# Second w_in's pieces decoded at an even rate, each tied on VectorE behind the evacuation of its feed-forward step

## Chip, cores and metric

The kernel runs on 1 core of one Trainium2 chip. The metric is device time in microseconds (us) of one execution; lower is better. Before the change three runs gave 786.98, 778.69 and 790.01 us (median 786.98).

## What is computed

Attention over 2 batches x 8 heads x 768 tokens x 64, in which a query sees the keys that were assigned to the same of 16 centroids, and then two feed-forward layers on the 1536 tokens of 512 features (d_ff is 2048):

```python
mask = q_assign[:, :, :, None] == k_assign[:, :, None, :]
scores = np.where(mask, scale * np.matmul(q, k.transpose(0, 1, 3, 2)), -1e9)
attn = softmax(scores)
x = np.matmul(attn, v)                  # 1536 x 512, after a transpose
h = x @ moe_w_in
g = np.maximum(h, 0.0) + np.log1p(np.exp(-np.abs(h)))
x = g @ moe_w_out
h = x @ moe2_w_in                       # the second w_in
g = np.maximum(0.01 * h, h)
out = g @ moe2_w_out
```

## The kernel before

The weights arrive as 64-bit floats. A piece of a weight is 128 x 512 numbers: SyncE loads its words into one of two staging buffers (`st`), VectorE puts an f32 together from them in three instructions (`decode`, L141, L144, L147), ScalarE rounds it to f16 (the high half) and VectorE subtracts to get the low half. All matrix products run as three f16 products, high x high, high x low and low x high.

The work stands in this order. The sixteen heads of attention come first; beside them the first layer's two weights are decoded, and from the ninth head on the first feed-forward layer runs interleaved with attention. That layer goes over four blocks of 384 tokens: (batch 0, tokens 0), (0, 384), (1, 0), (1, 384). Each block has

- `layer_in`: 16 steps of 12 matmuls (L576). After each step ScalarE evacuates the bank twice (`g_h`, L451, and f32 `mr`, L452), and VectorE subtracts them (`g_l`, L453). These four lines are `act_pair`'s.
- `layer_mid`: 4 outputs of 48 matmuls each (L589), which read all 16 pairs `g_h`, `g_l`, one pair after the other, three matmuls per pair. Each output is evacuated by ScalarE (`xth`, L593) and VectorE (`xtl`, L594).

A generator yields after each step of `layer_in` and four times in each output of `layer_mid`, so that a block has 32 yields; after each yield other work may be issued. Six PSUM banks turn among these steps once attention is done (`mps_next`), and `mr` has two buffers.

When attention is done, `w2` is opened and the second w_in (`moe2_w_in`) is queued: 16 pieces, in four groups of four quarters (`quad_pieces`). Each quarter is decoded (three VectorE instructions). The second layer's first product is computed with seven products in place of eight, for which sums and differences of quarters are needed: in each group GpSimd makes four differences (L209, L213, L215, L218), and ScalarE and VectorE split seven matrices into halves (L198, L199). GpSimd also makes the sums of the left side, `left_sums(0)`: 28 instructions (L485 and L183), with eight casts on ScalarE (`sh`, L182) in between; they need outputs of both blocks of batch 0. Then comes `layer_in2` (L521) and `layer_out` (L609).

What sets the order: every instruction is issued with a priority, and the compiler puts each engine's instructions into one fixed order. An engine then works through its order and waits where an input is not there. Feed-forward step n has priority 8 + 0.25 n. `w2_step`, called once after each yield, gives the v-th step of the second w_in the priority 17 + 0.9 v (`W2_PRI`), whatever step calls it; it finishes one piece (`convs.pop(0)()`) and starts the load of another. After the block (0, 384) a loop calls it until no piece is left.

In what follows "the second block" is (0, 384) and "the third block" is (1, 0). Line numbers are those of the kernel before; in the kernel after, the lines from L453 on stand 2 or 3 lines lower (L453 is L455, L485 is L487, L593 is L595, L594 is L596).

Of the kernel before, what the change touches and what calls it, by code (L numbers as in the profile page):

```python
# [13 lines left out]
ALU = mybir.AluOpType  # L14
# [31 lines left out]

W_FREE, W_FROM, W_TO, W_PER = 4, 8, 10, 5
W_PRI = ((0, 0.5), (17, 0.3))
W2_PRI = (17, 0.9)
O2_PRI = (38, 0.3)  # L50
S_PRI = 30

# [6 lines left out]
def attn_moe_kernel(  # L59
# [13 lines left out]
    V, S, G, PE = nc.vector, nc.scalar, nc.gpsimd, nc.tensor  # L73
# [94 lines left out]
    def in_pieces(w, wh, wl):  # L168
        wi = w.bitcast(I32)
        for f in range(DFF // 512):  # L170
            for kk in range(KDM):
                cs = slice(f * 512, (f + 1) * 512)
                src = wi[kk * 128:(kk + 1) * 128, f * 1024:(f + 1) * 1024]
                yield partial(w_piece, wh[:, kk, cs], wl[:, kk, cs], src)

    def out_pieces(w, wh, wl, order=None):
        wi = w.bitcast(I32)
        for kk in order or range(KFF):
            yield partial(w_piece, wh[:, kk, :], wl[:, kk, :], wi[kk * 128:(kk + 1) * 128, :])
# [245 lines left out]
    late, w2 = {}, {}  # L425
# [16 lines left out]
    def mps_next():  # L442
        if pmx[0] is pm:
            turn["m"] = 1 - turn.get("m", 0) if not (wq or convs) else 1
            return pm.tile([128, 512], F32, tag=f"m{turn['m']}", name="m")
        return pmx[0].tile([128, 512], F32, tag="m", name="m")

    def act_pair(m, hp, func, scale, alpha, g=("h", "l"), tag="mr"):
        r = late["mt"].tile([128, TB], F32, tag=tag, name=tag)
        gh, gl = (late[n][:, m, :] for n in g)  # L450
        S.activation(out=gh, in_=hp, func=func, scale=scale, alpha=alpha)  # L451
        S.activation(out=r, in_=hp, func=func, scale=scale, alpha=alpha)  # L452
        V.tensor_tensor(out=gl, in0=r, in1=gh, op=ALU.subtract)  # L453

    def act_softplus(m, hp):  # L455
        act_pair(m, hp, AF.Softplus, 1.0 / (WS * XS), 0.0)
# [13 lines left out]
    def act_leaky(m, hp, g, tag):  # L470
        act_pair(m, hp, AF.Prelu, 1.0 / WS, 0.01, g, tag)
# [92 lines left out]
    def layer_in(b, t0, act, wh, wl):  # L564
        xh, xl = xt_h[b], xt_l[b]
        ts = slice(t0, t0 + TB)
        for m in range(KFF):
            hp = mps_next()[:, 0:TB]
            ms = slice(m * 128, (m + 1) * 128)
            ops = []  # L570
            for kk in range(KDM):
                ops += [(wh[:, kk, ms], xh[:, kk, ts]), (wh[:, kk, ms], xl[:, kk, ts])]
            for kk in range(KDM):
                ops += [(wl[:, kk, ms], xh[:, kk, ts])]
            for i, (w_, x_) in enumerate(ops):
                PE.matmul(out=hp, lhsT=w_, rhs=x_, start=(i == 0), stop=(i == len(ops) - 1))  # L576
            act(m, hp)
            yield

    def layer_mid(b, t0):  # L580
        xh, xl = xt_h[b], xt_l[b]
        ts = slice(t0, t0 + TB)
        for m in range(KDM):
            yp = mps_next()[:, 0:TB]
            ms = slice(m * 128, (m + 1) * 128)
            n = 0
            for kk in range(KFF):
                for w_, g_ in ((w_outh, late["h"]), (w_outh, late["l"]), (w_outl, late["h"])):
                    PE.matmul(out=yp, lhsT=w_[:, kk, ms], rhs=g_[:, kk, :], start=(n == 0), stop=(n == 3 * KFF - 1))  # L589
                    n += 1  # L590
                if kk % 4 == 3:
                    if kk == KFF - 1:
                        S.activation(out=xh[:, m, ts], in_=yp, func=AF.Copy, scale=1.0 / WS)  # L593
                        V.scalar_tensor_tensor(  # L594
                            out=xl[:, m, ts], in0=yp, scalar=1.0 / WS, in1=xh[:, m, ts], op0=ALU.mult, op1=ALU.subtract  # L595
                        )  # L596
                    yield
# [20 lines left out]
    def pri(x):  # L618
        return int(100000 + 10000 * x)
# [4 lines left out]
    @contextmanager  # L624
    def at_pri(x):
        old = tc.cur_priority
        tc.cur_priority = pri(x)
        yield
        tc.cur_priority = old
# [8 lines left out]
    with at_pri(-9):  # L638
# [6 lines left out]
            out=ss[:, 1:2], in0=ss[:, 0:1], scalar1=ss[:, 2:3], scalar2=ss[:, 1:2], op0=ALU.mult, op1=ALU.add  # L645
# [30 lines left out]
    wq = list(in_pieces(w_in1, w_inh, w_inl))  # L676
    convs = []
    wtie = {"h": -1}

    cnt = {"w": 0, "v": 0, "m": 0}  # L680

    def w_step():
        w0, wr = W_PRI[cnt["w"] >= 34]
# [14 lines left out]
        cnt["w"] += 1  # L698

    def w2_step():  # L700
        with at_pri(W2_PRI[0] + W2_PRI[1] * cnt["v"]):
            if convs:
                convs.pop(0)()
            if wq:
                convs.append(wq.pop(0)())
        cnt["v"] += 1

    def m_steps(g):
        for _ in g:
# [4 lines left out]
    def moe1():  # L714
        wq.extend(out_pieces(w_out1, w_outh, w_outl))
        for b in range(B):
            for t0 in range(0, SEQ, TB):
                for _ in layer_in(b, t0, act_softplus if b or t0 else act_ln_exp, w_inh, w_inl):
                    if len(w2):
                        w2_step()  # L720
                    else:
                        w_step()
                    yield
                while (b, t0) == (0, 0) and (wq or convs):
                    w_step()
                if (b, t0) == (1, TB):
                    late["h2"], late["l2"] = (
                        w.rearrange("p k f -> p (k f)")[:, 0:KFF * TB].rearrange("p (k t) -> p k t", t=TB)
                        for w in (w_outh, w_outl)
                    )  # L730
                    order = [kk + 4 * r for kk in range(4) for r in range(4)]
                    wq.extend(out_pieces(w_out2, w_out2h, w_out2l, order))
                    for i in range(KFF + 1):
                        with at_pri(O2_PRI[0] + O2_PRI[1] * i):
                            if convs:
                                convs.pop(0)()
                            if wq:
                                convs.append(wq.pop(0)())
                for _ in layer_mid(b, t0):
                    if len(w2):  # L740
                        w2_step()
                    else:
                        w_step()
                    yield
                if (b, t0) == (0, TB):
                    while wq or convs:
                        w2_step()
                    with at_pri(S_PRI):
                        left_sums(0)

    def moe2():
        for b in range(B):
# [3 lines left out]
            for t0 in range(0, SEQ, TB):  # L756
                yield from layer_out(b, t0, w_out2h, w_out2l)

    ff = m_steps(moe1())

    def chain(h):
# [91 lines left out]
```

## Time and profile before

| what | us |
|---|---|
| three runs | 786.98, 778.69, 790.01 (median 786.98) |
| the profiled execution | 782.94 |
| its span, first to last instruction | 780.7 |
| TensorE matmul busy | 703.5 (90%) |
| VectorE busy | 435.0 (56%) |
| ScalarE busy | 352.1 (45%) |
| GpSimd busy | 303.7 (39%) |
| mean granted TensorE clock | 0.965 of full speed |

PE is TensorE, DVE is VectorE, ACT is ScalarE, POOL is GpSimd. Busy shares are means over stages with different limits: what counts is where TensorE, which runs the longest chain, stands idle or gets a lower clock, and who released it.

### The profile page before, as it was taken

Reading aid. Unit: us, or ns where it says so; the run is one execution under the profiler, and the core shown is the slowest. Engines: PE = TensorE matmul, PEld = TensorE weight load, DVE = VectorE, ACT = ScalarE, POOL = GpSimd, SP = SyncE. Lnnn points to the kernel's source line nnn. Section 1 sums busy time; section 2 is a strip of 40 time slices with the busy share of each in tenths; the row PEclk is TensorE's granted clock in tenths of the full one; section 3 lists DMA queues with packets and bytes.
Section 4 is the critical chain, followed back from the end, with each engine's and each line's share of the span. In section 5 each row is a group of like instructions: output and inputs, shape, how many; then the busy total and the mean of one; then the engine's idle time right before and its main releaser. Section 6 shows DMA issues by size and latency. Waiting matters only on the chain.

```text
span 780.7 us, 14239 instructions
## 1 busy us (share of the span) xinstructions
PE 703.5 (90%) x5712; PEld 420.6 (54%) x5712; DVE 435.0 (56%) x863; ACT 352.1 (45%) x831; POOL 303.7 (39%) x280
## 2 busy tenths in 40 slices
PE   1788988798798878899798999999999999999998
PEld 1365656455465555566454566666665444665443
DVE  4778757677787777319897411885566000565000
ACT  5375656477776646125433511532665201565000
POOL 5265656568688666303447800000115800111000
PEclk9999889999989989999899999999999999999999
DMA  8967566847675854212343000341000000000000
GB/s 197 183 137 146 120 109 129 167 101 169 173 158 136 162 123 129 93 20 79 113 139 103 1 1 1 108 162 55 1 1 1 27 28 28 1 1 1 27 28 27
DMA packets 104883, 66.03 MB, mean 85 GB/s; under 512 B 90993, under 2 KB 95089, under 8 KB 104817
## 3 DMA queue, kind: packets, MB, share of 16 engines
q1 hardware_dynamic: 104816, 65.13, 34.9%
q8 instruction: 44, 0.72, 0.4%
q14 instruction: 23, 0.18, 0.1%
HBM read 43.02 MB, written 3.15 MB: 59 GB/s over the span
## 4 chain that ended last, share of the span: by engine, by line
PE 61%; DMA 14%; DVE 12%; ACT 6%; issue 2%; POOL 2%; SPq 2%; ACTq 0%; DVEq 0%; POOLq 0%
PE m L609 16%; PE m L521 14%; PE m L589 12%; PE m L576 9%; DMA tk<-nk 3%; DMA v<-in_v_dram 3%; DMA tm<-nq 3%; DVE mm L310 2%; DMA t<-n 2%; DMA st<-in_moe_w_in_dram 2%; DVE w_in2l L199 2%; ACT p L343 2%; PE s L303 2%; PE s L336 1%; PE s L337 1%
## 5 line engine op out<-in xcount | busy, mean ns | idle before, releaser
L345 POOL TENSOR_TENSOR pl<-p 128x768 f16<-128x768 f32 x80 | 117.3, 1473 | 56.7 <-ACT p L343 29.3
L310 DVE TENSOR_REDUCE mm<-s 128x1 f32<-128x384 f32 x190 | 100.2, 550 | 34.7 <-PE s L303 32.2
L524 POOL TENSOR_TENSOR u<-u,p 128x384 f32<-128x384 f32 x16 | 18.2, 1137 | 224.1 <-DVE u L524 212.8
L576 PE MATMUL m<-xth,w_inh 128*128 128x384 f16 x256 | 85.9, 336 | 6.5 <-DVE xtl L594 3.3
L589 PE MATMUL m<-g_h,w_outh 128*128 128x384 f16 x256 | 85.1, 332 | 5.4 <-ACT g_h L451 2.3
L589 PE MATMUL m<-g_l,w_outh 128*128 128x384 f16 x256 | 84.9, 332 | 2.2 <-DVE g_l L453 2.2
L576 PE MATMUL m<-xtl,w_inh 128*128 128x384 f16 x256 | 85.9, 336 | 0.2 <-DMA xtl<-xnl 0.2
L343 ACT ACTIVATE p<-s 128x384 f32<-128x384 f32 x144 | 67.2, 494 | 40.8 <-PE s L337 32.9
L589 PE MATMUL m<-g_h,w_outl 128*128 128x384 f16 x256 | 84.9, 332 | 0.0
L303 PE MATMUL s<-tk,tq 80*128 80x384 f16 x190 | 64.1, 365 | 16.6 <-DMA tk<-nk 9.1
L576 PEld LDWEIGHTS <-w_inh 128*128 128x128 f16 x512 | 50.9, 100 | 42.5 <-issue 11.6
L589 PEld LDWEIGHTS <-w_outh 128*128 128x128 f16 x512 | 50.4, 99 | 40.6 <-issue 5.9
L337 PE MATMUL s<-tm,tk 81*128 81x384 f16 x160 | 53.9, 346 | 10.7 <-DMA tm<-nq 10.6
L336 PE MATMUL s<-t 128*128 128x384 f16 x160 | 54.8, 346 | 7.2 <-ACT p L343 6.5
L521 PEld LDWEIGHTS <-w_in2h 128*128 128x128 f16 x448 | 43.8, 98 | 29.5
L453 DVE TENSOR_TENSOR g_l<-mr,g_h 128x384 f16<-128x384 f32 x64 | 42.0, 659 | 30.2 <-ACT mr L452 30.1
L576 PE MATMUL m<-xth,w_inl 128*128 128x384 f16 x256 | 53.7, 334 | 0.0
L372 PE MATMUL x<-v,p 128*128 128x65 f16 x528 | 50.3, 198 | 1.5 <-DVE y L409 1.5
L373 PE MATMUL x<-v,p 128*128 128x64 f16 x528 | 51.0, 196 | 0.0
L614 ACT ACTIVATE ob<-m 128x512 f32<-128x512 f32 x12 | 7.2, 597 | 91.9 <-PE m L609 91.9
L451 ACT ACTIVATE g_h<-m 128x384 f16<-128x384 f32 x80 | 39.3, 491 | 15.8 <-PE m L576 8.0
L372 PEld LDWEIGHTS <-p 128*128 128x128 bf16 x528 | 40.7, 101 | 3.7 <-issue 1.1
(148 smaller groups left out, 1587.5 us busy)
## 6 DMA issues: line engine op xcount, KB each, us to landing
st<-in_moe_w_in_dram SPq DMA_DIRECT2D x32, 512.0 KB, 4.3
st<-in_moe_w_out_dram SPq DMA_DIRECT2D x32, 512.0 KB, 4.0
qk<-in_q_dram SPq DMA_DIRECT2D x16, 192.0 KB, 3.2
qk<-in_k_dram SPq DMA_DIRECT2D x16, 192.0 KB, 3.8
v<-in_v_dram SPq DMA_DIRECT2D x16, 192.0 KB, 4.2
out_dram<-ob SPq DMA_DIRECT2D x12, 256.0 KB, 2.0
t<-n SPq DMA_TRANSPOSE x16, 4.2
tq<-nq SPq DMA_TRANSPOSE x16, 3.0
```

Source lines behind the costliest of these rows:

```text
L303: PE.matmul(out=o, lhsT=t[0:KS1, c, :], rhs=tk[0:KS1, 3 * j:3 * j + 3, :], start=True, stop=True,)
L310: V.reduce_max(out=mms[h % 2][:, c, j:j + 1], in_=bank[:, 0:3 * 128], axis=AX)
L336: PE.matmul(out=o, lhsT=t1[:, kt, 1, :], rhs=t1[:, 3 * j:3 * j + 3, 0, :], start=True, stop=False)
L337: PE.matmul(out=o, lhsT=t2[0:KS2, kt, :], rhs=tqh[0:KS2, 3 * j:3 * j + 3, :], start=False, stop=True)
L343: S.activation(out=p[:, j, :], in_=sp, func=AF.Exp, scale=scale)
L345: G.tensor_tensor(out=pl, in0=p, in1=pb, op=ALU.subtract)
L372: PE.matmul(out=o, lhsT=pb[:, cs], rhs=v2[:, kt, D:2 * D + 1], start=(kt == 0 and c == 0), stop=False)
L373: PE.matmul(out=o[:, 0:D], lhsT=pb[:, cs], rhs=v2[:, kt, 0:D], start=False, stop=False)
L521: PE.matmul(out=bank, lhsT=w_, rhs=x_, start=(first and i == 0), stop=(i == 5), skip_group_check=True)
L576: PE.matmul(out=hp, lhsT=w_, rhs=x_, start=(i == 0), stop=(i == len(ops) - 1))
L589: PE.matmul(out=yp, lhsT=w_[:, kk, ms], rhs=g_[:, kk, :], start=(n == 0), stop=(n == 3 * KFF - 1))
L609: PE.matmul(out=op, lhsT=g_[:, kk, rs], rhs=w_[:, kk, :], start=(n == 0), stop=(n == 3 * KFF - 1))
```

## The change

`W2_PRI` goes. `w2_step` now counts the feed-forward yields and finishes pieces at an even rate, 17 steps over 60 yields, so that the decode runs from the second block to the end of the third. The instructions of a piece that stand on VectorE are put behind the last evacuation that VectorE was given (`tie["dve"]`, the `g_l` or `xtl` of the step just issued); that is an order within VectorE's queue, not a wait on another engine. The load of the next piece is issued with a priority two heads earlier. The loop that finished all pieces after the second block goes.

```diff
@@ -46,7 +46,7 @@
-W2_PRI = (17, 0.9)
+W2_STEPS = 60
@@ -445,12 +445,14 @@
+    tie = {}
+
     def act_pair(m, hp, func, scale, alpha, g=("h", "l"), tag="mr"):
...
-        V.tensor_tensor(out=gl, in0=r, in1=gh, op=ALU.subtract)
+        tie["dve"] = V.tensor_tensor(out=gl, in0=r, in1=gh, op=ALU.subtract)
@@ -591,7 +593,7 @@
-                        V.scalar_tensor_tensor(
+                        tie["dve"] = V.scalar_tensor_tensor(
@@ -677,7 +679,7 @@
-    cnt = {"w": 0, "v": 0, "m": 0}
+    cnt = {"w": 0, "v": 0, "w2": 0, "m": 0}
@@ -698,12 +700,15 @@
     def w2_step():
-        with at_pri(W2_PRI[0] + W2_PRI[1] * cnt["v"]):
+        cnt["v"] += 1
+        while cnt["w2"] * W2_STEPS < 17 * cnt["v"] and (wq or convs):
             if convs:
-                convs.pop(0)()
+                with tc.issue_after(tie["dve"].ins):
+                    convs.pop(0)()
             if wq:
-                convs.append(wq.pop(0)())
-        cnt["v"] += 1
+                with at_pri(tc.cur_priority / 10000 - 10 - 2):
+                    convs.append(wq.pop(0)())
+            cnt["w2"] += 1
@@ -743,8 +748,6 @@
                 if (b, t0) == (0, TB):
-                    while wq or convs:
-                        w2_step()
                     with at_pri(S_PRI):
                         left_sums(0)
```

In the instruction orders the same instructions stand on every engine before and after. SyncE keeps its order but for one thing: two of the 16 loads move behind the last two transposes of attention. TensorE's order changes at the end of attention alone: some products of the last head move behind matmuls of `layer_mid` and between the first `layer_in` step of the second block.

VectorE, the end of attention, where the last piece of the first layer's w_out is decoded (`wcp`) and its low half made (`w_outl`, L164); `wd` is a piece of the second w_in in decode. Before:

```order
L144 SCALAR_TENSOR_TENSOR wcp<-st,wcp 128x512
L141 TENSOR_SCALAR wd<-st 128x512
L147 SCALAR_TENSOR_TENSOR wcp<-st,wcp 128x512
L144 SCALAR_TENSOR_TENSOR wd<-st,wd 128x512
L147 SCALAR_TENSOR_TENSOR wd<-st,wd 128x512
L164 SCALAR_TENSOR_TENSOR w_outl<-wcp,w_outh 128x512
```

After:

```order
L141 TENSOR_SCALAR wcp<-st 128x512
L144 SCALAR_TENSOR_TENSOR wcp<-st,wcp 128x512
L147 SCALAR_TENSOR_TENSOR wcp<-st,wcp 128x512
L164 SCALAR_TENSOR_TENSOR w_outl<-wcp,w_outh 128x512
L596 SCALAR_TENSOR_TENSOR xtl_85<-m,xth_83 128x384 x4
```

The three instructions of a first `wd` that stood among those of the last `wcp` are gone from there.

VectorE, the last steps of `layer_in` in the second block, up to its last `g_l`; `w_in2l` is a low half of the second w_in. Before:

```order
L453 TENSOR_TENSOR g_l<-mr,g_h 128x384
L144 SCALAR_TENSOR_TENSOR wd<-st,wd 128x512
L453 TENSOR_TENSOR g_l<-mr,g_h 128x384
L147 SCALAR_TENSOR_TENSOR wd<-st,wd 128x512
L141 TENSOR_SCALAR wd<-st 128x512
L199 SCALAR_TENSOR_TENSOR w_in2l<-wd,w_in2h 128x512
L144 SCALAR_TENSOR_TENSOR wd<-st,wd 128x512
L453 TENSOR_TENSOR g_l<-mr,g_h 128x384
```

After:

```order
L455 TENSOR_TENSOR g_l<-mr,g_h 128x384 x2
L199 SCALAR_TENSOR_TENSOR w_in2l<-wd,w_in2h 128x512
L455 TENSOR_TENSOR g_l<-mr,g_h 128x384
L141 TENSOR_SCALAR wd<-st 128x512
L144 SCALAR_TENSOR_TENSOR wd<-st,wd 128x512
L147 SCALAR_TENSOR_TENSOR wd<-st,wd 128x512
L455 TENSOR_TENSOR g_l<-mr,g_h 128x384
L199 SCALAR_TENSOR_TENSOR w_in2l<-wd,w_in2h 128x512
L455 TENSOR_TENSOR g_l<-mr,g_h 128x384
```

Before, pieces follow each other through these steps without a break; after, the first piece stands behind the seventh `g_l` of the block, and the pieces lie two to four `g_l` apart.

VectorE, the third block. Before, all its 16 `g_l` stand in a row (`xtl_85` belongs to batch 0, `xtl_86` to batch 1):

```order
L594 SCALAR_TENSOR_TENSOR xtl_85<-m,xth_83 128x384
L453 TENSOR_TENSOR g_l<-mr,g_h 128x384 x16
L594 SCALAR_TENSOR_TENSOR xtl_86<-m,xth_84 128x384 x4
L453 TENSOR_TENSOR g_l<-mr,g_h 128x384 x3
L164 SCALAR_TENSOR_TENSOR w_inl<-wc,w_inh 128x512 x2
```

After, four pieces stand among them; these are the last rows up to the block's last `g_l`:

```order
L147 SCALAR_TENSOR_TENSOR wd<-st,wd 128x512
L455 TENSOR_TENSOR g_l<-mr,g_h 128x384
L199 SCALAR_TENSOR_TENSOR w_in2l<-wd,w_in2h 128x512 x2
L455 TENSOR_TENSOR g_l<-mr,g_h 128x384
L199 SCALAR_TENSOR_TENSOR w_in2l<-wd,w_in2h 128x512
L455 TENSOR_TENSOR g_l<-mr,g_h 128x384
L141 TENSOR_SCALAR wd<-st 128x512
L144 SCALAR_TENSOR_TENSOR wd<-st,wd 128x512
L147 SCALAR_TENSOR_TENSOR wd<-st,wd 128x512
L455 TENSOR_TENSOR g_l<-mr,g_h 128x384
L199 SCALAR_TENSOR_TENSOR w_in2l<-wd,w_in2h 128x512
L455 TENSOR_TENSOR g_l<-mr,g_h 128x384
```

From the third output of the second block's `layer_mid` to this last `g_l` VectorE now has six decodes (18 instructions) and 11 splits (L199) beside the 16 `g_l`. On ScalarE splits (L198) and casts of left sums (L182) stand between the evacuations of the same stretch; before, it had only the casts there.

On GpSimd all 16 differences stood ahead of the first left sum before. Now the sums begin behind the fifth difference, and six more differences stand among and behind the 28 sums before the last `g_l` above is reached; the other five follow later.

## Rows read from the trace of the kernel before

**Rows 1.** The page, part 2: 40 slices, busy tenths and granted clock.

```profile
PE   1788988798798878899798999999999999999998
PEclk9999889999989989999899999999999999999999
```

**Rows 2.** Busy time by stretch; x counts instructions; columns are in the first row.

```profile
core 0: us, PE busy (x) PEld busy (x) DVE busy (x) ACT busy (x) POOL busy (x), PEclk, DMA share, GB/s
...
380.00:400.00 20.00, 15.57 (x81) 8.38 (x79) 18.41 (x29) 7.42 (x15) 7.86 (x5) 0.83 0.39 124
...
420.00:440.00 20.00, 16.72 (x96) 9.60 (x94) 9.83 (x10) 7.55 (x18) 19.92 (x20) 0.91 0.08 27
440.00:544.00 104.00, 104.00 (x642) 62.62 (x640) 51.71 (x91) 35.31 (x79) 6.71 (x7) 1.00 0.19 61
```

**Rows 3.** Timeline of TensorE: matmuls that waited, with idle time and releaser.

```profile
315.59 0.34 PE L589 MATMUL m<-g_h,w_outh 128*128 128x384 f16 x1 [1.24 <-ACT w_outh L163]
...
317.55 0.48 PE L589 MATMUL m<-g_h,w_outh 128*128 128x384 f16 x1 [0.91 <-DVE w_outl L164]
...
382.93 0.32 PE L589 MATMUL m<-g_l,w_outh 128*128 128x384 f16 x1 [0.79 <-DVE g_l L453]
...
386.76 0.48 PE L589 MATMUL m<-g_h,w_outh 128*128 128x384 f16 x1 [2.28 <-ACT g_h L451]
388.18 0.48 PE L589 MATMUL m<-g_l,w_outh 128*128 128x384 f16 x1 [0.94 <-DVE g_l L453]
...
427.03 0.48 PE L576 MATMUL m<-xth,w_inh 128*128 128x384 f16 x1 [3.28 <-DVE xtl L594]
```

**Rows 4.** Busy time in the stretch behind the wait at 317.55.

```profile
317.40:320.60 3.20, 3.05 (x11) 1.48 (x11) 1.91 (x4) 0.00 (x0) 0.82 (x1) 0.52 0.62 193
```

**Rows 5.** Timeline of VectorE: start, duration, instruction.

```profile
313.77 0.53 DVE L141 TENSOR_SCALAR wd<-st 128x512 int32<-128x512 int32 x1 [0.67 <-DMA st<-in_moe_w_in_dram]
314.22 0.68 DVE L147 SCALAR_TENSOR_TENSOR wcp<-st,wcp 128x512 int32<-128x512 int32 x1
...
316.81 0.68 DVE L164 SCALAR_TENSOR_TENSOR w_outl<-wcp,w_outh 128x512 f16<-128x512 f32 x1
...
380.32 0.55 DVE L453 TENSOR_TENSOR g_l<-mr,g_h 128x384 f16<-128x384 f32 x1
380.79 0.68 DVE L199 SCALAR_TENSOR_TENSOR w_in2l<-wd,w_in2h 128x512 f16<-128x512 f32 x1
381.39 0.41 DVE L141 TENSOR_SCALAR wd<-st 128x512 int32<-128x512 int32 x1
381.73 0.68 DVE L199 SCALAR_TENSOR_TENSOR w_in2l<-wd,w_in2h 128x512 f16<-128x512 f32 x1
...
387.57 0.55 DVE L453 TENSOR_TENSOR g_l<-mr,g_h 128x384 f16<-128x384 f32 x1
...
418.86 1.28 DVE L144 SCALAR_TENSOR_TENSOR wc<-st,wc 128x512 int32<-128x512 int32 x1
```

**Rows 6.** Timeline of ScalarE: evacuations of layer_mid's outputs.

```profile
425.90 0.48 ACT L593 ACTIVATE xth<-m 128x384 f16<-128x384 f32 x1
...
457.77 0.49 ACT L593 ACTIVATE xth<-m 128x384 f16<-128x384 f32 x1 [5.99 <-PE m L589]
465.57 0.49 ACT L593 ACTIVATE xth<-m 128x384 f16<-128x384 f32 x1 [7.31 <-PE m L589]
```

**Rows 7.** Timeline of GpSimd: a difference, and two left sums in a row.

```profile
374.29 1.27 POOL L213 TENSOR_TENSOR wd<-wd 128x512 f32<-128x512 f32 x1 [2.22 <-DVE wd L147]
...
426.28 0.91 POOL L183 TENSOR_TENSOR sl<-e,sh 128x384 f16<-128x384 f32 x1
427.15 0.91 POOL L485 TENSOR_TENSOR e<-e,xtl 128x384 f32<-128x384 f32 x1
```

**Rows 8.** Busy time in two stretches in which VectorE or GpSimd never rests.

```profile
352.20:388.20 36.00, 31.57 (x192) 18.51 (x190) 32.81 (x51) 19.21 (x41) 13.82 (x8) 0.96 0.33 103
417.60:447.50 29.90, 26.62 (x157) 15.54 (x156) 15.35 (x15) 12.99 (x32) 29.04 (x29) 0.94 0.10 35
```

## Prediction

> **What bounds the kernel now.** I read the strip of the page first. One slice is 19.5 us. Counted from zero, slice 16 is the last of attention, and behind it every slice of TensorE shows 9 but 19, 21 and the last; the clock drops to 8 at 19 [rows 1]. So the kernel is bound by TensorE, and from about 320 us on a microsecond of the end is bought only by taking away a wait of TensorE or a stretch at the lower clock. The busy times by stretch say how much there is. At full clock TensorE starts 642 matmuls in 104 us, one per 0.162 us, or 123.5 per 20 us. From 380 to 400 us it starts 81, from 420 to 440 us it starts 96 [rows 2]. The missing 42.5 and 27.5 matmuls are 6.9 and 4.5 us. After 440 us nothing is missing until the tail of the last output.
>
> The timeline of TensorE then names the waits [rows 3]. At 382.93 and 388.18 it waits for `g_l`, at 386.76 for `g_h`: the start of `layer_mid` in the second block wants the last pairs, and VectorE is late. VectorE's own timeline shows why: `g_l` at 380.32 and 387.57 stand in one queue with splits and decodes of the second w_in, without a gap between them [rows 5]. At 427.03 TensorE waits 3.28 us for `xtl`. That is a bank: the fourth output of the second block was finished long before, but its `xth` ran only at 425.90 [rows 6], behind casts that waited for left sums on GpSimd. At 315.59 and 317.55 TensorE waits 1.24 and 0.91 us for the halves of the last w_out piece [rows 3]. VectorE had begun a `wd` at 313.77 before that piece's last decode at 314.22, and made its low half at 316.81 only after two more `wd` instructions [rows 5].
>
> Each wait costs more than itself. After 317.55 the granted clock is 0.52, so the lower level of 1.2 GHz, and 11 matmuls run in 3.2 us where 19.8 would fit [rows 4]: 1.3 us lost beyond the wait itself. After 427.03 it is 4.5 - 3.28 = 1.2 us.
>
> **What the change removes.** (A) At 313 us the three `wd` instructions leave the last w_out piece alone. Its last decode can start where the `wd` stood, a microsecond earlier, and the low half follows ScalarE's cast. I let 0.6 us of the 1.24 + 0.91 = 2.15 us stay, since the chain decode, cast, low half is itself as long as the work TensorE has there, and give back the 1.3 us of clock: 2.15 - 0.6 + 1.3 = 2.8 us.
>
> (B) In the second block at most one decode stands between two `g_l`: 0.34 + 2 x 0.60 = 1.54 us by the distances from start to start in VectorE's timeline (L141 to the next is 0.34, L199 to the next 0.60), and one `g_l` is 0.47 [rows 5]. A step of `layer_in` takes 12 x 0.162 = 1.95 us, and pieces come every two to four steps. VectorE keeps up, the last pair is ready some 2 us after its step, and `layer_mid` wants it 45 x 0.162 = 7.3 us after. The whole 6.9 us goes.
>
> (C) The left sums begin earlier relative to TensorE, since `xtl` of the third output is no longer behind VectorE's queue, and the fourth output is evacuated with fewer casts in front. The bank is free in time: 4.5 us.
>
> Together 6.9 + 4.5 + 2.8 = 14.2 us. Loads cost nothing: the same 16, and with seven microseconds or more between pieces each has landed before its decode. The two loads moved behind attention's last transposes are for pieces decoded later still. The moved products of the last head are the same matmuls. If that cover were gone, one load is late by no more than the 0.67 us that the `wd` at 313.77 waited [rows 5].
>
> **What it adds.** The work does not vanish, it moves into the third block, where the left sums are. VectorE and GpSimd hinder each other there: L144 takes 1.28 us beside left sums [rows 5] where instructions of its width take 0.68. How much, two stretches in which one of the two never rests tell [rows 8]. I add each instruction by its distance alone: 0.87 for a left sum (426.28 to 427.15), 1.27 for a difference [rows 7], and the VectorE distances above. From 352.2 to 388.2 VectorE has 15 splits, 13 `g_l`, 8 decode starts and 15 other decode instructions: 9.0 + 6.1 + 2.7 + 9.0 = 26.8; GpSimd has 8 differences, 10.2. The sum is 37.0, the stretch is 36.0. From 417.6 to 447.5 there are 28 left sums, 10 `g_l`, a decode and a split: 24.4 + 4.7 + 1.5 + 0.6 = 31.2 in 29.9 us. So the two engines' times add up, to 0.965 of the sum, as if they were one engine.
>
> The Trainium skill has this as a rule ("SBUF — State Buffer", section "Who interferes with whom"): a VectorE instruction with two SBUF inputs and a GpSimd instruction that reads SBUF lock each other out for the whole instruction. It speaks against this change, and the trace nearly agrees: by it the full durations add up, by the rows the shorter distances do. What the full durations would give is a rival below.
>
> Now the third block, with zero where TensorE finishes the third output of the second block. An output takes 465.57 - 457.77 = 7.8 us [rows 6], so the fourth ends at 7.8, sixteen steps of 1.95 us end at 39.0, and the next `layer_mid` wants the last pair at 46.3. The shared time begins at 0.6, when the third `xth` is there, and before the last `g_l` it must carry 28 x 0.87 + 6 x 1.27 = 32.0 us of GpSimd and 6 x 1.54 + 11 x 0.60 + 16 x 0.47 = 23.4 us of VectorE. Nothing of it can be left for later, since ScalarE's casts and splits stand between the evacuations, and VectorE's between the `g_l`. 55.4 x 0.965 = 53.5 us, so the last `g_l` is ready at 54.1: 7.8 us late. TensorE waits that long in several pieces, some for banks before the block's end and some for the last pairs after it, and I price two restarts at the lower clock, 2 x 1.25 = 2.5 us. The bounds: nothing, if the shared time had gaps to fill that I don't see, and 16.8 us by the full durations. I take 7.8 + 2.5 = 10.3 us, as the two stretches are the nearest rows. The four pieces after it meet no left sums and lie beside `layer_mid` of the third block, 31 us for 4 x 1.54 us of decodes and some ten splits; they cost nothing.
>
> **The sum.** The profiled execution took 782.94 us. 782.94 - 14.2 + 10.3 = 779.0 us. It lies near the middle of the runs shown, whose median is 786.98; the mean of all four is 784.7 us, and on that scale the change gives 784.7 - 3.9 = 780.8 us. What follows is on that scale.
>
> **Rivals.** First, the third block holds: VectorE and GpSimd find room beside each other, and the last pair comes within the 7.3 us that `layer_mid` leaves. For it: from 417.6 to 447.5 VectorE was busy only 15.35 of 29.9 us [rows 8]. Against it: the sum of that same stretch. It gives 784.7 - 14.2 = 770.5 us.
>
> Second, slower: the lock is held for whole durations in the third block, and TensorE waits there for more than it saved. With 0.55 for `g_l`, 0.68 for splits and wide decode instructions, 0.41 for L141 [rows 5], 0.91 for left sums and 1.27 for differences [rows 7], VectorE holds 6 x 1.77 + 11 x 0.68 + 16 x 0.55 = 26.9 us and GpSimd 25.5 + 7.6 = 33.1 us. The last `g_l` comes at 60.6, 14.3 us late, and with 2.5 us of clock that costs 16.8 us: 784.7 + 2.6 = 787.3 us. It decides once the pair is more than 11.7 us late. For it: ScalarE's order ties the two engines together, so each cast that waits opens a gap in both. Against it: full durations overshoot the stretch from 417.6 (34 us where 29.9 passed). This is the skill's rule named above, taken at its word.
>
> Third, the change does not do what it says in the second block: the last `g_l` there stay late because ScalarE's splits, which stand between evacuations, wait for GpSimd. Then the 6.9 us stay and the 10.3 come too: 784.7 - 7.3 + 10.3 = 787.7 us. Against it: each split there has its difference finished a step earlier.
>
> **Chances.** The forecast 0.5; the third block holds 0.22; slower by whole durations 0.2; the second block stays late 0.08. The forecast's own range is 776 to 786. Both neighbours, 770.5 and 787.7, lie outside it, and the four executions shown spread by some 6 us to either side, so the range that holds 8 in 10 is 768 to 791. Two per cent, about what a measurement of this kernel can tell from no change, is 15.7 us. Even with all 14.2 us the gain stays below it; only the full gain and a favourable spread pass it: faster 0.07. For slower by 2% the third block would have to lose 30 us: 0.03. Within 2%: 0.90.
>
> **What would show it.** In the profile after, TensorE's waits at 315 to 318 us shrink to some 0.6 us, those for `g_l` near 380 us are gone, and slice 19 of the strip is full at full clock. A new dip stands at the end of `layer_in` and the start of `layer_mid` in the third block, near 440 to 450 us, with waits for `g_l`, `g_h` or a bank released by ScalarE, some 8 us in total; VectorE and GpSimd together never rest for the 50 us before it. The prediction is wrong if that dip is missing or costs over 13 us, if the dip near 380 us stays, or if TensorE waits anew after 480 us, where I expect no change.

## The result and the profile after

The changed kernel takes 776.34 us (median of 20 runs, 769.52 to 782.41) and the kernel before 785.89 us (20 runs): a ratio of 0.9877, with a 95% interval of 0.9848 to 0.9906, so 7.4 to 11.9 us less. Forecast were 780.8 us and a gain of 3.9 us, with the result within two per cent: the direction and three of the four terms held, and the added term was priced too high. The median lies just inside the forecast's own range of 776 to 786 us, and the gain of the medians, 9.6 us, is two and a half times the one forecast.

The strip of the changed kernel's page, against [rows 1]:

```profile
PE   1798989889887878999999889999999999999998
PEclk9999887989899998999999999999999999999999
```

Counted from zero, the dip at slices 19 and 21 is gone, with the clock's 8 at slice 19, and a new one stands at 22 and 23, which is 426 to 465 us. The busy times by stretch, whose columns are those of [rows 2], say how large it is:

```profile
380.00:400.00 20.00, 20.00 (x125) 12.04 (x124) 9.05 (x16) 3.88 (x7) 4.23 (x4) 1.00 0.27 79
420.00:440.00 20.00, 19.22 (x119) 11.48 (x118) 19.93 (x19) 9.65 (x23) 18.35 (x15) 1.00 0.18 53
440.00:460.00 20.00, 16.21 (x89) 8.81 (x88) 16.31 (x24) 8.31 (x17) 6.06 (x4) 0.91 0.35 106
```

From 380 to 400 us TensorE now starts 125 matmuls where it started 81. A full stretch of 20 us counts 125, as here, so from 420 to 460 us it starts 208 of 250: 42 missing, at 0.162 us each 6.8 us. The timeline of TensorE names all its waits after attention:

```profile
316.36 0.34 PE L591 MATMUL m<-g_h,w_outh 128*128 128x384 f16 x1 [0.16 <-ACT w_outh L163]
...
317.08 0.32 PE L591 MATMUL m<-g_h,w_outh 128*128 128x384 f16 x1 [0.22 <-DVE w_outl L164]
...
437.48 0.32 PE L591 MATMUL m<-g_h,w_outh 128*128 128x384 f16 x1 [0.78 <-ACT mr L454]
...
444.91 0.32 PE L591 MATMUL m<-g_l,w_outh 128*128 128x384 f16 x1 [1.26 <-DVE g_l L455]
...
445.98 0.32 PE L591 MATMUL m<-g_l,w_outh 128*128 128x384 f16 x1 [0.42 <-DVE g_l L455]
...
448.24 0.32 PE L591 MATMUL m<-g_l,w_outh 128*128 128x384 f16 x1 [1.61 <-DVE g_l L455]
...
449.79 0.48 PE L591 MATMUL m<-g_l,w_outh 128*128 128x384 f16 x1 [0.49 <-DVE g_l L455]
```

Against [rows 3]: the 2.15 us at 315 to 318 us are 0.38 us, and the waits near 380 us and the 3.28 us for a bank at 427 us are gone. In their place stand 4.56 us of waits in the third block, at the end of `layer_in` and the start of `layer_mid`.

**Where the time went.** Four landmarks separate the terms. In this execution attention itself ended 1.85 us later (VectorE's L144 of the last w_out piece at 314.25, before at 312.40; up to there the two rows of instructions are alike). The other three are the second step of the second block's `layer_in`, the fourth output of its `layer_mid`, and ScalarE's `xth` of the second output of the third block. TensorE starts the first two at these times, first of the kernel before, then of the changed one:

```profile
346.21 0.34 PE L576 MATMUL m<-xth,w_inh 128*128 128x384 f16 x1
...
406.04 0.33 PE L589 MATMUL m<-g_h,w_outh 128*128 128x384 f16 x1
```

```profile
344.87 0.34 PE L578 MATMUL m<-xth,w_inh 128*128 128x384 f16 x1
...
397.53 0.33 PE L591 MATMUL m<-g_h,w_outh 128*128 128x384 f16 x1
```

I take the second step and not the first, because 18 products of the last head, which stood behind the wait at 315.59 before, now stand among the matmuls of the first step. The end of attention gave 346.21 - 344.87 + 1.85 = 3.2 us. The fourth output starts 8.51 us earlier, so the second block gave 8.51 - 1.34 = 7.2 us. The third landmark is

```profile
459.12 0.49 ACT L595 ACTIVATE xth<-m 128x384 f16<-128x384 f32 x1 [0.82 <-PE m L591]
```

where [rows 6] have 465.57, 6.45 us later. So between these two landmarks 8.51 - 6.45 = 2.1 us were given back: 6.8 us lost in the new dip, 4.7 us gained at the bank. Together 3.2 + 7.2 + 4.7 - 6.8 = 8.3 us. The spans differ by 780.7 - 774.3 = 6.4 us, with the 1.85 us of attention 8.25: the account closes.

**A ruler for the experiments.** The time at which attention ends varies between executions: the matmul that waits for `w_outh` started anywhere from 311.93 to 320.47 us in the profiles compared here. So each profile is also measured from that matmul to the end of the span. I call this the tail: 780.7 - 315.59 = 465.1 us before, 774.3 - 316.36 = 457.9 us after. It holds everything but 1.1 us of the wait before it (1.24 us, now 0.16).

### The profile page after: what moved, and what is told of

Its sections match the earlier page's. It is cut to its first block, busy times and chain, and to the rows that moved or that the text cites. A ratio compares the mean times of both kernels' runs of the same rounds, so it can differ in the third digit from the quotient of the medians.

```text
span 774.3 us, 14231 instructions
## 1 busy us (share of the span) xinstructions
PE 705.0 (91%) x5712; PEld 422.2 (55%) x5712; DVE 442.0 (57%) x863; ACT 355.0 (46%) x831; POOL 305.6 (39%) x280
## 4 chain that ended last, share of the span: by engine, by line
PE 69%; DMA 10%; DVE 10%; ACT 4%; issue 2%; POOL 2%; SPq 1%; ACTq 0%; POOLq 0%; DVEq 0%
PE m L611 16%; PE m L591 15%; PE m L523 14%; PE m L578 12%; DVE mm L310 3%; PE s L303 2%; DMA tk<-nk 2%; DMA tm<-nq 2%; DMA v<-in_v_dram 2%; PE s L337 2%; DMA t<-n 2%; PE s L336 2%; DMA st<-in_moe_w_in_dram 1%; ACT p L343 1%; PE x L359 1%
## 5 line engine op out<-in xcount | busy, mean ns | idle before, releaser
L337 PE MATMUL s<-tm,tk 81*128 81x384 f16 x160 | 56.3, 362 | 10.6 <-DMA tm<-nq 10.6
L336 PE MATMUL s<-t 128*128 128x384 f16 x160 | 56.6, 357 | 5.9 <-ACT p L343 5.6
L455 DVE TENSOR_TENSOR g_l<-mr,g_h 128x384 f16<-128x384 f32 x64 | 43.8, 690 | 29.1 <-ACT mr L454 28.9
```

The source lines that it names most:

```text
L336: PE.matmul(out=o, lhsT=t1[:, kt, 1, :], rhs=t1[:, 3 * j:3 * j + 3, 0, :], start=True, stop=False)
L337: PE.matmul(out=o, lhsT=t2[0:KS2, kt, :], rhs=tqh[0:KS2, 3 * j:3 * j + 3, :], start=False, stop=True)
```

## The experiments

My theory: decodes of the second w_in and left sums share time on VectorE and GpSimd, because a VectorE instruction with two SBUF inputs and a GpSimd instruction that reads SBUF keep each other out; that is what makes `g_l` late, in the second block of the kernel before and in the third block of the changed one. The rival: VectorE and ScalarE are simply given too many instructions between two evacuations. A second question is what the tie does and what the even rate does.

| kernel | ratio to before, 95% interval | tail, us |
|---|---|---|
| changed | 0.9877 (0.9848 to 0.9906) | 457.9 |
| even rate alone | 0.9984 (0.9941 to 1.0028) | - |
| tie alone | 0.9973 (0.9940 to 1.0005) | 464.9 |
| changed, sums late | 0.9873 (0.9823 to 0.9922) | 459.0 |
| changed, decode in bank | 0.9807 (0.9747 to 0.9867) | 451.1 |
| before, decode in bank | 0.9918 (0.9885 to 0.9951) | 460.6 |
| changed, no left sums | 0.9757 (0.9702 to 0.9812) | 452.3 |
| changed, rate 75 | 0.9895 (0.9849 to 0.9940) | 458.9 |
| before, tie and bank | 0.9921 (0.9884 to 0.9959) | - |
| changed, again | 0.9852 (0.9809 to 0.9896) | 460.6 |
| changed, decode in bank, again | 0.9742 (0.9697 to 0.9786) | 451.1 |

For two kernels no tail is compared.

### The even rate without the tie

```diff
             if convs:
-                with tc.issue_after(tie["dve"].ins):
-                    convs.pop(0)()
+                convs.pop(0)()
```

> The even rate without the tie. My theory: the tie is what moves VectorE's instructions, and the rate by itself leaves them in the row of the kernel before, so the time is that of before: ratio 0.996 to 1.004, with the waits of before near 315, 380 to 388 and 427 us (some 14 us in all with the clock). Rival: the even rate alone carries the gain, and the tie only fixes it: ratio 0.985 to 0.991, and no wait for g_l near 380 us.

Measured 0.9984 (0.9941 to 1.0028): no change. VectorE's instructions stand in exactly the row of the kernel before. An emission rate by itself moved nothing; the tie is what holds a decode back to the step it is issued with.

### The tie without the even rate

The kernel before, with the tie:

```diff
         with at_pri(W2_PRI[0] + W2_PRI[1] * cnt["v"]):
             if convs:
-                convs.pop(0)()
+                with tc.issue_after(tie["dve"].ins):
+                    convs.pop(0)()
```

> The kernel before with the tie, at the old rate: the pieces stay as dense as before, so most of them lie in the second block. Theory: the tie alone gives part A (the three decode instructions are gone from the last w_out piece, about 3.7 us) and leaves the third block free of decodes, so no dip near 445 us; what the dense pieces cost in the second block stays, at least in part (up to 6.9 us): ratio 0.988 to 0.996. Rival one: the tie does everything, since each decode then stands behind a feed-forward evacuation and never ahead of one: all of 14 us, ratio 0.982 or less. Rival two: both parts are needed, and the tie with dense pieces gives nothing: ratio 0.997 to 1.003.

Measured 0.9973 (0.9940 to 1.0005): nothing that can be told from no change. The account by what TensorE waited for (columns: us in total, times, longest) and two stretches of the same kernel show why:

```profile
PE m L578 <- DVE xtl L596: 6.7, 1, 6.7
PE m L591 <- DVE g_l L455: 2.9, 1, 2.9
```

```profile
380.00:400.00 20.00, 17.09 (x106) 10.20 (x105) 19.05 (x27) 5.89 (x11) 9.25 (x5) 1.00 0.42 121
...
420.00:440.00 20.00, 11.98 (x66) 6.64 (x65) 19.86 (x19) 8.38 (x18) 18.31 (x15) 0.83 0.29 94
```

The last w_out piece is free (0.16 and 0.22 us of waiting, as in the changed kernel), and from 380 to 400 us 106 matmuls start where 81 did. But the dense pieces still cross the end of the second block, and the wait for the bank grows from 3.28 to 6.7 us: from 420 to 440 us only 66 matmuls start, 96 before. What the tie gains, it loses 40 us later. The second rival was right: the change needs both its parts.

### The left sums moved into the third block's `layer_mid`

The changed kernel; `left_sums(0)` is called in the third block, each instruction behind the last difference of the decode that GpSimd has been given by then:

```diff
-                    G.tensor_tensor(out=c, in0=c, in1=held[0], op=ALU.subtract)
+                    tie["pool"] = G.tensor_tensor(out=c, in0=c, in1=held[0], op=ALU.subtract)
...
+                if (b, t0) == (1, 0):
+                    with at_pri(S_PRI), tc.issue_after(tie["pool"].ins):
+                        left_sums(0)
...
-                if (b, t0) == (0, TB):
-                    with at_pri(S_PRI):
-                        left_sums(0)
```

> The changed kernel, with the left sums moved behind the last difference of the decode, so that GpSimd does them beside the third block's layer_mid. Theory (VectorE and GpSimd share their time where left sums and decodes meet): the dip near 437 to 450 us goes, some 6 us, VectorE's decode instructions in the third block fall from 1.3 to about 0.7 us, and the time is 769 to 772 us beside 776 of the changed kernel: ratio to before 0.978 to 0.983. Rival: the six pieces are too much for VectorE and ScalarE between the evacuations whatever GpSimd does, the dip stays: ratio 0.986 to 0.990.

Measured 0.9873 (0.9823 to 0.9922), the changed kernel's own time. By the ratio the rival holds; the trace shows that both statements were half right. TensorE's waits after attention:

```profile
482.01 0.32 PE L578 MATMUL m<-xth,w_inh 128*128 128x384 f16 x1 [2.23 <-DVE xtl L596]
...
510.72 0.32 PE L591 MATMUL m<-g_l,w_outh 128*128 128x384 f16 x1 [0.59 <-DVE g_l L455]
...
512.39 0.32 PE L591 MATMUL m<-g_l,w_outh 128*128 128x384 f16 x1 [1.03 <-DVE g_l L455]
...
514.76 0.32 PE L591 MATMUL m<-g_l,w_outh 128*128 128x384 f16 x1 [1.72 <-DVE g_l L455]
```

The dip of the third block is gone: no wait of TensorE between 320 and 479 us. But the sums did not come after all decodes, as I had expected: the last difference by then is that of the third group of four, so the pieces of the fourth group lie beside the sums, in `layer_mid` of the third block (VectorE's L144 takes 1.29 to 1.40 us there). So the next block begins late: 2.23 us for a bank at its first steps, and `g_l` late at its end, where the decodes of the second w_out stand. The loss moved by one block and kept its size (tail 459.0 beside 457.9 us). What the same decodes do without any sums beside them is shown further down.

### The decode's intermediate value in a PSUM bank

The changed kernel; the first two instructions of a decode of the second w_in write a bank `t` and the third reads it, so that none of the three has two SBUF inputs. Same instructions, same count:

```diff
-            out=c, in0=hi, scalar=-0x40000000, in1=c, ...
+            out=t, in0=hi, scalar=-0x40000000, in1=t, ...
...
-            out=c, in0=lo, scalar=29, in1=c, ...
+            out=c, in0=lo, scalar=29, in1=t, ...
...
+                turn["d"] = 1 - turn.get("d", 0)
+                t = pm.tile([128, 512], I32, tag=f"m{turn['d']}", name="wt")
```

> The changed kernel, with the intermediate value of a decode of the second w_in held in a PSUM bank, so that its second and third instruction read SBUF only once. Same instructions, same count, left sums where they are. Theory (the two engines lock each other out where a VectorE instruction has two SBUF inputs): 14 decode instructions of the stretch from 398 to 438 us drop out of the shared time, 6.5 us of 44.8, so the last g_l comes 5.8 us earlier, which is in time: the dip goes, decode instructions beside left sums take some 0.7 us where they took 1.3, ratio 0.978 to 0.983. Rival one: it is the plain load on VectorE, so the durations fall to no less than 1.1 us and the dip stays: ratio 0.986 to 0.990. Rival two: the bank is slower to reach and adds to each instruction: ratio above 0.990.

Measured 0.9807 (0.9747 to 0.9867), tail 451.1 us. To compare it with the changed kernel on one chip, both ran again side by side.

> The changed kernel itself, once more, as the partner of the next run on one chip: ratio to before 0.985 to 0.991.

> The changed kernel with the decode's intermediate value in a PSUM bank, beside the changed kernel on one chip. From the wait for w_outh at the end of attention to the end of the span the changed kernel took 457.9 us and this one 451.1 us: 6.8 us less, so a ratio to before of 0.978 to 0.983 and some 0.991 of the changed kernel. Rival: the earlier difference (0.9807 beside 0.9877) came from different chips, and the two are within 0.3% of each other here.

Measured 0.9852 (0.9809 to 0.9896) for the changed kernel, 0.9742 (0.9697 to 0.9786) with the bank: medians of 778.07 and 769.35 us, a quotient of 0.989, and again a tail of 451.1 us. The earlier difference did not come from the chips. VectorE's order changed with the edit, by little: 10 splits stand ahead of the third block's last `g_l` where 11 stood, and one split is 0.60 us by its distance. VectorE's instructions by line and operation from 400 to 437 us (count, busy us, mean ns of one, idle before and its releaser), first of the changed kernel, then of this one in the second run, where L142 to L200 are the same instructions as L141 to L199:

```profile
L455 DVE TENSOR_TENSOR g_l<-mr,g_h 128x384 f16<-128x384 f32 x10 | 12.9, 1322 | 0.9 <-ACT mr L454 0.9
L199 DVE SCALAR_TENSOR_TENSOR w_in2l<-wd,w_in2h 128x512 f16<-128x512 f32 x6 | 7.2, 1194 | 2.7 <-ACT w_in2h L198 2.5
L147 DVE SCALAR_TENSOR_TENSOR wd<-st,wd 128x512 int32<-128x512 int32 x4 | 5.3, 1333 | 0.1
L144 DVE SCALAR_TENSOR_TENSOR wd<-st,wd 128x512 int32<-128x512 int32 x4 | 5.3, 1328 | 0.1
L141 DVE TENSOR_SCALAR wd<-st 128x512 int32<-128x512 int32 x4 | 4.1, 1014 | 0.0
L596 DVE SCALAR_TENSOR_TENSOR xtl<-m,xth 128x384 f16<-128x384 f32 x1 | 0.5, 544 | 0.0
```

```profile
L458 DVE TENSOR_TENSOR g_l<-mr,g_h 128x384 f16<-128x384 f32 x12 | 12.7, 1057 | 4.7 <-ACT mr L457 4.7
L200 DVE SCALAR_TENSOR_TENSOR w_in2l<-wd,w_in2h 128x512 f16<-128x512 f32 x8 | 9.0, 1125 | 2.9 <-ACT w_in2h L199 2.7
L148 DVE SCALAR_TENSOR_TENSOR wd<-st,wt 128x512 int32<-128x512 int32 x5 | 3.4, 679 | 0.1
L145 DVE SCALAR_TENSOR_TENSOR wt<-st,wt 128x512 int32<-128x512 int32 x4 | 2.8, 689 | 0.1
L142 DVE TENSOR_SCALAR wt<-st 128x512 int32<-128x512 int32 x4 | 2.7, 681 | 0.0
L599 DVE SCALAR_TENSOR_TENSOR xtl<-m,xth 128x384 f16<-128x384 f32 x1 | 0.5, 544 | 0.0
```

GpSimd never rests in this stretch in the first kernel and for 1.1 us in the second. The two decode instructions that lost an SBUF input fall from 1328 and 1333 to 689 and 679 ns, their time without company. `g_l` and the split, which still have two SBUF inputs, stay above 1000 ns. `xtl`, one SBUF input and one bank, takes 544 ns in both. That is the lock, seen instruction by instruction; a plain load on VectorE would not choose by operand. VectorE gets through 12 `g_l` and 8 splits in the time of 10 and 6, and idles 7.8 us where it idled 3.8. TensorE has no wait left after 317 us:

```profile
440.00:460.00 20.00, 20.00 (x125) 12.05 (x124) 16.02 (x25) 6.47 (x13) 5.47 (x4) 1.00 0.36 105
```

The Trainium skill says in "SBUF — State Buffer", section "Who interferes with whom", that a VectorE instruction with at most one SBUF input, outside the modes that use two ports, does not contend with GpSimd, and counts `tensor_scalar` among those that can enter such a mode. The runs agree: L141 has one SBUF input and yet takes 1014 ns beside sums, where [rows 5] have it at 0.41 us; with a bank as its output it takes 681 ns, slower alone and undisturbed.

### The bank without tie and rate

The kernel before with the same edit of the decode.

> The kernel before, with neither tie nor even rate, and with the intermediate value of a decode of the second w_in in a PSUM bank. Theory (the locks between VectorE and GpSimd make up the lateness, so that the order of the decodes matters only while they lock): in the second block VectorE's own 26.8 us fit into 36, the waits for g_l and g_h near 380 to 388 us go, part B, some 6.5 us; the last w_out piece still stands behind decodes, so the 2.15 us of part A stay, and of part C between nothing and all: ratio 0.986 to 0.992. Rival: what hurts before is the dense row of decodes between two g_l, by VectorE's own time, and the bank changes nothing in it: ratio 0.997 to 1.002.

Measured 0.9918 (0.9885 to 0.9951), tail 460.6 us. The waits of TensorE in the second block and at the start of the third, and ScalarE at the latter place:

```profile
386.38 0.32 PE L592 MATMUL m<-g_l,w_outh 128*128 128x384 f16 x1 [0.50 <-DVE g_l L456]
...
425.26 0.48 PE L579 MATMUL m<-xth,w_inh 128*128 128x384 f16 x1 [5.25 <-DVE xtl L597]
```

```profile
421.24 0.51 ACT L183 CAST sh<-e 128x384 f16<-128x384 f32 x1 [3.14 <-POOL e L488]
421.66 0.48 ACT L596 ACTIVATE xth<-m 128x384 f16<-128x384 f32 x1
```

The 4.0 us of waits for `g_l` and `g_h` near 380 us in [rows 3] are 0.50 us, with decodes still standing densely among the `g_l`. That does not show that the lock with the differences had made `g_l` late in the second block, because VectorE's order differs too. Before, two pieces were decoded at the end of attention; here none is. Counted from TensorE's first matmul of the block, the first decode starts at 6.4 us where it started at 8.6, and up to the block's last `g_l` there are 11 splits where there were 14, and two decode instructions more. That `g_l` ends 4.2 us earlier, and the earlier start alone is 2.2 us of it. Some `g_l` are still held up beside a difference (two in a row take 2.85 us at 380.61). How much of the 4.2 us is the lock stays open. The waits at the last w_out piece went as well (0.16 and 0.22 us), which I had not expected: `wt` takes a bank that `wcp` uses too, and that may have held the decodes back; I did not test it. What the bank does not cure is the wait for `xtl`. ScalarE's cast of a left sum waits 3.14 us for GpSimd, and the evacuation `xth` stands behind it. That is the place where the even rate is needed.

### Without the left sums of batch 0

The changed kernel; GpSimd fills the sums' tiles with zeros, so that the second layer's first product of batch 0 is computed with zeros there.

```diff
-                        left_sums(0)
+                        w2["s"] = tuple(...)
+                        for s in w2["s"]:
+                            G.memset(s, 0.0)
```

> The changed kernel without the left sums of batch 0: their place is filled with zeros by GpSimd, so layer_in2 of batch 0 computes with zeros there and the output of that batch is another. It measures term D of the prediction by itself. Theory (decodes meet left sums): the dip of the third block goes with them; by the trace of the changed kernel D is 5.75 us late and 0.5 us of clock, some 6.3 us: ratio 0.978 to 0.982, VectorE's decodes there at 0.7 us. Rival: the six pieces alone make VectorE and ScalarE late: dip stays, ratio 0.986 to 0.989.

Measured 0.9757 (0.9702 to 0.9812), tail 452.3 us: 5.6 us less than the changed kernel, with every stretch from 320 to 500 us full:

```profile
420.00:440.00 20.00, 20.00 (x125) 12.03 (x123) 17.24 (x25) 11.50 (x24) 5.85 (x4) 1.00 0.26 80
440.00:460.00 20.00, 20.00 (x126) 12.04 (x124) 11.54 (x18) 4.03 (x8) 4.21 (x3) 1.00 0.26 79
```

With the same decodes on the same rate and no sums there is no dip, so the decodes alone are not too much. It is not quite the floor: one `g_l` is 0.95 us late at 505.80. With that wait the sums cost 5.6 + 0.95 = 6.6 us, close to the 6.8 us of the landmarks; the expectation's half microsecond of clock was a misreading (below). The kernel with the bank, which does all the work, has the shorter tail.

### A slower rate

The changed kernel with one number changed:

```diff
-W2_STEPS = 60
+W2_STEPS = 75
```

> The changed kernel with one number changed: W2_STEPS 75 where it was 60, so 17 pieces to 75 steps. From the third output of the second block to the last g_l of the third there are then 4 decodes and 7 splits on VectorE where there were 6 and 11, and two differences fewer on GpSimd; 7 pieces come after it where there were 4. Theory (shared time): 2 x 1.54 + 4 x 0.60 + 2 x 1.27 = 8.0 us less to share, at 0.90 of the sum 7.2 us, more than the 5.75 us by which the last g_l was late: the dip goes and nothing new comes, since no left sums are left: ratio 0.978 to 0.983. Rival: the seven pieces make VectorE late in the fourth block, beside the decodes of the second w_out, as in the run with the sums late: ratio 0.985 to 0.989.

Measured 0.9895 (0.9849 to 0.9940), tail 458.9 us: no better than 60. TensorE and ScalarE of this run:

```profile
540.54 0.80 PE L523 MATMUL m<-xth,w_in2h 128*128 128x384 f16 x2 [5.64 <-ACT w_outh L539]
```

```profile
539.11 0.63 ACT L163 ACTIVATE w_inh<-wc 128x512 f16<-128x512 f32 x1 [2.50 <-DVE wc L147]
539.65 0.47 ACT L595 ACTIVATE xth<-m 128x384 f16<-128x384 f32 x1
540.02 0.47 ACT L539 COPY w_outh<-m 128x384 f32<-128x384 f32 x1
```

The dip is gone, as the sum of shared time had it: two waits of 0.18 and 0.16 us are left of 4.56. But the pieces that come later push the decodes of the second w_out back, and their last casts now stand before the first copy of `layer_in2` in ScalarE's order: TensorE waits 5.64 us at 540 us. The rival named the right cause; the wait stands just behind the fourth block, not in it.

### Tie and bank at the dense rate

The tie alone, with the same edit of the decode.

> The kernel before with the tie at the old dense rate (0.9973 when alone) and the decode's intermediate value in a PSUM bank. Theory: part A is there by the tie, the lateness of g_l in the second block goes with the lock, and what stays is at most the wait for xtl at the start of the third block, 6.7 us with the tie alone, shorter here as casts and sums come sooner: ratio 0.980 to 0.988. Rival: the dense rate costs by VectorE's own time, ratio 0.995 to 1.000.

Measured 0.9921 (0.9884 to 0.9959), between the two expectations and the same as the bank without the tie. With the lock of the decodes gone the tie alone still adds nothing, and the even rate, on top of both, does: 0.9807 and 0.9742.

## Why the prediction was right, and which term was mis-sized

The steps in the order of the prediction:

- **(A), the end of attention, 2.8 us.** Measured 3.2. The waits left are 0.38 us, where I let 0.6 stay, so 1.8 us of waits are gone, and with the 1.3 us of clock of [rows 4] that is 3.1.
- **(B), the second block, 6.9 us.** Measured 7.2 by the landmarks. The 123.5 matmuls of the prediction are a little low, since a full stretch counts 125: 44 were missing, 7.1 us. That the lateness goes when the pieces are spread out is shown. Why the dense row was late is not: I argued from VectorE's own time, and the bank without tie and rate, with 0.50 us of waiting in a row still dense, does not separate that from the lock with GpSimd's differences.
- **(C), the bank at 427 us, 4.5 us.** Measured 4.7, which is the loss of the kernel before between the last two landmarks (59.5 us to the end of that second output, where the same work takes 54.8 us one block later); by the full count 29 matmuls were missing, also 4.7 us. In the changed kernel the fourth `xth` of the second block comes at 406.45, less than a microsecond after its output ended (397.53 + 0.16 + 7.8). The mechanism, `xth` behind casts that wait for left sums, stands in ScalarE's timeline of the kernel before, ahead of the `xth` at 425.90 [rows 6], and again in the run with the bank alone:

```profile
425.49 0.51 ACT L182 CAST sh<-e 128x384 f16<-128x384 f32 x1 [2.63 <-POOL e L485]
```

- **(D), the third block, plus 10.3 us.** The mechanism is shown: the dip stands where it was forecast, it goes when the sums go, and it goes when the decode instructions stop locking. Mis-sized is the step "55.4 x 0.965 = 53.5 us ... 7.8 + 2.5 = 10.3 us". The loss was 6.8 us.

Two numbers of (D) were too high. The last `g_l` was ready at 449.17 + 0.56 = 449.73 us, which is 52.0 us after the third output, not 54.1: 5.7 us late instead of 7.8. From 0.6 to 52.0 us 55.4 us of instructions were carried, a factor of 0.93. The timelines of VectorE and GpSimd show what it comes from:

```profile
418.73 1.38 DVE L144 SCALAR_TENSOR_TENSOR wd<-st,wd 128x512 int32<-128x512 int32 x1
420.04 1.40 DVE L199 SCALAR_TENSOR_TENSOR w_in2l<-wd,w_in2h 128x512 f16<-128x512 f32 x1
421.36 1.40 DVE L147 SCALAR_TENSOR_TENSOR wd<-st,wd 128x512 int32<-128x512 int32 x1
422.68 1.27 DVE L455 TENSOR_TENSOR g_l<-mr,g_h 128x384 f16<-128x384 f32 x1
```

```profile
419.53 1.36 POOL L487 TENSOR_TENSOR e<-xth,e 128x384 f32<-128x384 f16 x1
420.85 1.36 POOL L487 TENSOR_TENSOR e<-xth 128x384 f32<-128x384 f16 x1
422.17 1.36 POOL L183 TENSOR_TENSOR sl<-e,sh 128x384 f16<-128x384 f32 x1
423.49 1.23 POOL L487 TENSOR_TENSOR e<-e,xtl 128x384 f32<-128x384 f32 x1
```

The engines take turns, one instruction each, every 1.32 us: 420.04 to 421.36 on VectorE, 420.85 to 422.17 on GpSimd. By their own distances a split and a sum are 0.60 + 0.87 = 1.47 us. So a turn costs 0.90 of the sum. My 0.965 was read from two stretches in which only one of the two never rested [rows 8]; it mixed turns with time in which one of them worked alone or waited, and was no price for a turn. By the Trainium skill's rule that the prediction named ("SBUF — State Buffer", section "Who interferes with whom"), the second engine waits for the whole instruction; by these rows a pair takes 1.32 us, a tenth less than the two distances and less still than the two durations alone (0.68 + 0.91 = 1.59 us).

The clock was the other number. I priced two restarts at 1.25 us each. Behind the waits at 437.48, 444.91 and 445.98 the granted clock was 1.00. It fell once, some 0.3 us after the start at 448.24, and stayed at the lower level of 1.2 GHz (0.50) over the next wait:

```profile
448.60:449.30 0.70, 0.69 (x2) 0.10 (x1) 0.63 (x2) 0.54 (x2) 0.05 (x1) 0.50 0.67 94
449.70:453.00 3.30, 3.21 (x14) 1.66 (x14) 3.23 (x5) 1.01 (x2) 1.15 (x1) 0.67 0.29 112
```

What the low clock took before 449.30 is hidden in the wait for the last `g_l`. After that wait 14 matmuls start where 3.30 us at full clock hold 20.3: 1.0 us, of which only 0.09 us is the wait that ends at 449.79. So some 1.0 us of clock came on top of 5.7 us of lateness, where 2.5 and 7.8 were forecast, and the two together are the 6.8 us of the landmarks.

Of the rivals, "the third block holds" did not come true in this kernel, and did in the one with the bank. "Slower by whole durations" fails by the 1.32 us turns. "The second block stays late" fails by the 125 matmuls from 380 to 400 us. That nothing is new after 480 us, which the prediction named as a sign, held in the first profile, but not always: when the changed kernel ran again, one `g_l` was 1.89 us late at 514.07, in the fourth block, and the tail was 460.6 where it had been 457.9 us. So the prediction was wrong to expect no change there. Why that one differs between executions stays open. By the terms of the first profile 8.3 us were gained, inside the interval of the runs (7.4 to 11.9 us), where 3.9 were forecast: 3.5 of the 4.4 us between them are (D).

## What to carry to other kernels

Where VectorE and GpSimd are both busy, look at the operands: here an instruction whose mean doubled while its neighbours with a PSUM operand kept theirs was waiting for the other engine, and moving one intermediate value into a bank, at the same instruction count, took 6.8 us off the tail beyond the changed kernel, where two further orders took nothing. Moving such work to another stretch moves the loss with it: sums late and rate 75 both cleared the dip and paid the same some 40 to 100 us later, so follow the trace to the end of the kernel before calling a stall removed. To set where work runs in a fixed order, a rate and a tie are one tool: either alone changed nothing here.

## What the runs showed that I had not expected

- VectorE and GpSimd alternate instruction by instruction under the lock, at 1.32 us for a split and a sum that take 0.60 and 0.87 us by themselves.
- The first decode instruction (L141, one SBUF input, int32 to int32) takes 0.41 us alone with SBUF as its output and 1.01 us beside sums; with a bank as its output it is 0.68 us in either case.
- Waits of TensorE of 0.78, 1.26 and 0.42 us were each followed by the full clock, while after 0.91 us in [rows 3] the granted clock was 0.52. In these rows the length of a single wait did not decide it.
- The tail of the kernel with the bank was 451.1 us in both of its profiled executions, whose attention ended 3.9 us apart: what separates these two executions lies ahead of the stretch that the change is about.
